# Opening and first batch: queries' exponentials head by head with row sums, and the key fold placed later

## The chip, the cores and the metric

The kernel runs on one core of one Trainium2 chip. The metric is the time of one execution on the device in microseconds (us), the median over runs.

## The reference

One launch computes three layers for a batch of 8, with 8 heads, 576 positions and 64 elements per head (512 channels): a linear attention, a gated feed-forward layer with a mixing over positions, and a second layer with a low-rank mixing over positions and a wide feed-forward part.

```
q_s = exp(q - max(q, axis=-1));  q_s = q_s / (sum(q_s, axis=-1) + 1e-9)     # per row and head
k_s = exp(k - max(k, axis=2));   k_s = k_s / (sum(k_s, axis=2) + 1e-9)      # over positions
x = q_s @ (k_s.T @ v)                                                       # per head
h = gelu_tanh(x @ w_in);  u, v = halves of h                                # 512 -> 2 x 512
v_n = (v - mean) / sqrt(var + 1e-6) * g_ln                                  # per row
x = x + (u * (w_sg @ v_n + b_sg)) @ w_out
y = x + (U @ V).T mixed over positions
out = y + relu(y @ w_ch1) @ w_ch2                                           # 512 -> 2048 -> 512
```

The change touches only how `q_s` is made for the first two batches, and when the maximum over positions is taken for the keys of the second.

## The kernel before, in words

A batch is worked on in tiles of 128 positions (four of 128 and one of 64, `t` = 0 to 4). Matrix products are done in split precision: each operand is a high part (`h`, written by ScalarE as a copy) and a low part (`l`, the rest, written by VectorE or GpSimd), and a product is three matmuls.

Names: `qt` and `kt` are the query and key tiles of a batch; `qm` and `qs` the row maxima and row sums of the queries per head; `km` the maximum of the keys over the tiles (`k_fold`), which four TensorE transposes (`pm`) and a reduction turn into `mx` (`k_max`), and four more (`pb`, `k_spread`) spread over all partitions. `k_sub` subtracts it, `k_exp` takes the exponential. `pk` is the product of keys and values (`emit_kv`), `pt` the transposed queries (`emit_qT`, which gives `qh`, `ql`), `px` the attention's output (`emit_xT`: `xh`, `xl`). `pv` is the gated layer's second half (`emit_Vh`, gelu into `ge`, of which there are three buffers; then the row statistics and the normalization, `vh`, `vl`), `pu` its first half in four blocks `f` (`emit_Uh`, gelu into `ut`), `pS` the mixing over positions in four blocks (`emit_S`, into `gt`, split into `gh` and `gl`), `py` the output product (`emit_y`). `pt`, `px`, `pv`, `pu`, `pS` and `py` share three PSUM buffers in turn.

The weights come as float64 words, are loaded in pieces into `stg`, clamped (L171), scaled by ScalarE (L177), merged by VectorE (L183, L184) and split into high and low parts (`wih`/`wil`, `wo_h`/`wo_l`). Some pieces are put between the steps of every batch.

The orders: in the opening (first batch up to `px`) VectorE, ScalarE, GpSimd and SyncE work in the order of the code. In the loop over the batches TensorE and VectorE do; ScalarE and GpSimd get theirs from a scheduler at build time. In the pass of the loop for batch `b`, the queries and keys of batch `b` + 1 (`nxt`) are prepared: maxima behind the `pv` products (`Q_MAX`, `FOLDS`), subtractions behind the `pu` products (`Q_SUB`, `K_SUB`), exponentials after the fourth gelu of `pu`, sums and the division (`q_total`, `q_norm`: two tiles on VectorE and three on GpSimd for the second batch) before the first `pS`; then `pk`, two `pt` and the first `py` follow `pS` on TensorE.

Of the kernel before, what the change touches and what calls it, by code (L numbers as in the profile page):

```python
# [22 lines left out]
def fused_kernel(tc, q, k, v, w_in, g_ln, w_sgT, b_sg, w_out, U, V, w_ch1, w_ch2, outT):  # L23
# [30 lines left out]
    def tt(eng, out, a, b, op):  # L54
        return eng.tensor_tensor(out=out, in0=a, in1=b, op=op)  # L55
# [347 lines left out]
    def k_fold(b):  # L403

        kt = k_t[b]
        m = km_t[b] = att.tile([P, C], F32, tag="kh", name="km")
        tt(dve, m, kt[:, 0], kt[:, 1], ALU.max)
        yield
        for t in range(2, NT):
            yield tt(dve, m, m, kt[:, t], ALU.max)  # L410
        tt(dve, m, m, kt[:, NT], ALU.max)
        yield

    def k_max(b):
# [23 lines left out]
        for t in tiles:  # L438
            act.activation(kt[:, t], kt[:, t], AF.Exp)

    q_s = {}

    def q3(t):
        return qt[0 : TR[t], t].rearrange("p (h d) -> p h d", d=D)

    def q_max(b, t):
        if t == 0:
            q_s[b] = tmpp.tile([P, NT + 1, H], F32, tag="qm", name="qm")
        dve.tensor_reduce(
            out=q_s[b][0 : TR[t], t], in_=q3(t), op=ALU.max, axis=mybir.AxisListType.X  # L450
        )

    def q_sub(b, t, eng=dve):
        n = TR[t]
        tt(eng, q3(t), q3(t), q_s[b][0:n, t].unsqueeze(2).to_broadcast([n, H, D]), ALU.subtract)

    def q_exp(b, t):
        act.activation(qt[0 : TR[t], t], qt[0 : TR[t], t], AF.Exp)

    def q_sum(b, t):  # L460
        if t == 0:
            q_s[b] = tmpp.tile([P, NT + 1, H], F32, tag="qs", name="qs")
        s = q_s[b]
        dve.tensor_reduce(out=s[0 : TR[t], t], in_=q3(t), op=ALU.add, axis=mybir.AxisListType.X)

    def q_total(b):

        s = q_s[b]
        for part in (s[:, 0:NT], s[0:R, NT]):
# [29 lines left out]

    def norm_kv(b):  # L500
        pk = kv_t[b]
        rs = tmpp.tile([P, 16], F32, tag="rs", name="rs")[:, 0:NC]
        for rows, _, _, total, _ in PAIR:
            dve.tensor_scalar(
                out=rs[rows].unsqueeze(2), in0=pk[rows, :, total], scalar1=1e-9, scalar2=None, op0=ALU.add
            )
        dve.reciprocal(out=rs, in_=rs)
        for rows, keys, _, _, rest in PAIR:
            tt(dve, kv[rows, :, keys], pk[rows, :, rest], rs[rows].unsqueeze(2).to_broadcast([E, NC, E]), ALU.mult)
        kh = att.tile([P, NC, P], F32R, tag="kh", name="kh")  # L510
# [682 lines left out]
    K_SUB = (((), (), (0, 1, 2), (3, 4)), ((), (), (0,), (1, 2, 3, 4)))  # L1193
    Q_NORM_DVE = (2, 5)

    def borrowed(tag):
# [3 lines left out]
    with in_order(dve, act, pool, sp):  # L1200
        load_k(0)
        load_q(0)
        ahead = list(pieces)
        for piece in ahead[0:1]:
            piece.load()
        load_v(0)
        for piece in ahead[1:5]:
            piece.load()
        for piece, tag in zip(ahead[5:14], ("vh0", "vl0", "vh1", "vl1", "vh2", "vl2", "vh3", "vl3", "vh4")):
            piece.load(borrowed(tag))  # L1210
        sp.dma_start(gl, g_ln)
# [42 lines left out]
    for b in range(B):  # L1254
# [53 lines left out]
        for f in range(NF):  # L1308
            if nxt and f == spread_at:
                k_spread(nxt)  # L1310
            if b == 0:
                slot(TURNS[b][1][f])
            if not nxt:
                for _ in range((0, 2, 2, 2)[f]):
                    next(prep, None)
            emit_Uh(b, f)
            if f == 0:
                emit_ln(b, NT)
# [17 lines left out]
        if nxt:  # L1336
            with contextlib.nullcontext() if b else tc.issue_after(last['g', 3].ins):
                for t in range(NT + 1):
                    q_exp(nxt, t)
            with contextlib.nullcontext() if b else tc.issue_after(last['g', 3].ins):  # L1340
                k_exp(nxt)
            for t in range(NT + 1):
                q_sum(nxt, t)
            q_total(nxt)
            for t in range(NT + 1):
                q_norm(nxt, t, dve if t < Q_NORM_DVE[b > 0] else pool)
# [170 lines left out]
```

## Time and profile before

| | |
|---|---|
| median of 3 runs | 1309.66 us (1308.72 to 1312.9) |
| the profiled execution | 1311.05 us, of it 1309.2 us span from the first to the last instruction |
| TensorE busy | 1260.0 us, 96% of the span; granted clock 0.991 of full speed on average |
| VectorE, ScalarE, GpSimd busy | 969.0, 636.9 and 330.4 us |
| opening, up to the last `px` | 0 to 36.4 us |
| first pass of the loop: `pv`, `pu`, `pS`, `pk`/`pt`, `py` | from 36.4, 58.8, 74.9, 89.9 and 95.7 us |

Times of instructions are counted from the start of the span. A row of the timeline gives start and duration of one instruction, or of several alike that follow one another (x2), and in brackets the idle time of the engine before it and whose end it waited for. The durations come from the profiled execution, whose time is 1.4 us above the median.

### The profile page before, as it was taken

The page shows a single profiled execution, that of the slowest core. Times are in us where ns is not written, and L with a number is a line of the kernel's source. Part 1 is how long each engine was busy: PE and PEld are TensorE (multiplying, and loading weights), DVE is VectorE, ACT ScalarE, POOL GpSimd, SP SyncE. Part 2 cuts the span into 40 slices and gives each one's busy share as a digit, 9 for nine tenths or more (in the row PEclk, how much of TensorE's full clock was granted, in tenths as well). Part 3 has the DMA queues.
Part 4 walks back from the last instruction along what each step waited for, and adds up shares of the span by engine and source line. Part 5 has one row for each costly group of instructions (what it writes and reads, how often), then busy time and mean ns, then how long its engine had stood idle before and what let it go on. Part 6 is the DMA issues. An engine that isn't in the chain of part 4 may idle for free.

```text
span 1309.2 us, 20581 instructions
## 1 busy us (share of the span) xinstructions
PE 1260.0 (96%) x7592; PEld 1139.1 (87%) x7592; DVE 969.0 (74%) x1406; ACT 636.9 (49%) x979; POOL 330.4 (25%) x426
## 2 busy tenths in 40 slices
PE   4799999999999999898999999999999999999998
PEld 3598999999898989798888888888888889999998
DVE  7888879787988888788668953598337963694485
ACT  4756656575757466654454512444134422451342
POOL 4634152624243333665340202000010002000000
PEclk9899999999999999998999999999999999999999
DMA  8515171725343352468998667678756788899896
GB/s 268 164 47 171 37 218 37 225 70 167 96 151 120 111 168 73 162 208 299 312 344 315 227 231 257 209 242 290 257 193 226 243 285 297 269 304 315 260 290 215
DMA packets 135907, 274.14 MB, mean 209 GB/s; under 512 B 15232, under 2 KB 56704, under 8 KB 135808
## 3 DMA queue, kind: packets, MB, share of 16 engines
q1 hardware_dynamic: 135808, 272.84, 63.2%
q8 instruction: 60, 0.98, 0.3%
q14 instruction: 39, 0.32, 0.1%
HBM read 224.56 MB, written 48.23 MB: 208 GB/s over the span
## 4 chain that ended last, share of the span: by engine, by line
PE 79%; DVE 7%; DMA 4%; ACT 2%; issue 1%; POOL 1%; SPq 0%; DVEq 0%; ACTq 0%; POOLq 0%
PE mm L52 50%; PE pS L52 6%; PE pu L52 6%; PE pv L52 5%; PE py L52 5%; DMA stg<-in_w_ch_dram 1%; PE pm L52 1%; PE pp L52 1%; PE px L52 1%; PE pt L698 1%; DVE yt L55 1%; DVE f L183 1%; PE pk L52 1%; PE pt L527 1%; DMA wu<-wd 1%
## 5 line engine op out<-in xcount | busy, mean ns | idle before, releaser
L52 PE MATMUL mm<-oh,wu 128*128 128x512 f32 (+1 forms) x1120 | 320.7, 367 | 0.0
L52 PE MATMUL mm<-uh,wu 128*128 128x512 f32 (+1 forms) x1064 | 303.7, 366 | 1.9 <-DMA wu<-wd 1.1
L52 PEld LDWEIGHTS mm<-oh,wu 128*128 128x128 f32 x1120 | 207.0, 188 | 26.1
L52 PEld LDWEIGHTS mm<-uh,wu 128*128 128x128 f32 x1064 | 196.3, 188 | 26.4 <-issue 1.4
L52 PE MATMUL mm<-ol,wu 128*128 128x512 f32 (+1 forms) x560 | 205.7, 367 | 0.0
L61 ACT ACTIVATE oh<-h 128x1024 fp32r<-128x1024 f32 (+1 forms) x140 | 135.2, 973 | 124.8 <-PE mm L52 102.4
L52 PE MATMUL mm<-ul,wu 128*128 128x512 f32 (+1 forms) x532 | 194.9, 366 | 0.0
L55 DVE TENSOR_TENSOR ol<-h,oh 128x1024 fp32r<-128x1024 f32 (+1 forms) x140 | 155.4, 1113 | 40.9 <-ACT oh L61 40.1
L55 POOL TENSOR_TENSOR ust<-ust 128x1024 f32<-128x1024 f32 (+1 forms) x16 | 36.4, 2282 | 389.4 <-DMA ust<-u2d 348.8
L55 DVE TENSOR_TENSOR h<-mm,u 128x1024 f32<-128x1024 f32 (+1 forms) x57 | 63.3, 1111 | 87.8 <-PE mm L52 87.7
L52 PEld LDWEIGHTS mm<-ol,wu 128*128 128x128 f32 x560 | 105.2, 188 | 13.1
L55 DVE TENSOR_TENSOR u<-mm,u 128x1024 f32<-128x1024 f32 (+1 forms) x53 | 58.9, 1111 | 76.7 <-PE mm L52 71.3
L52 PEld LDWEIGHTS mm<-ul,wu 128*128 128x128 f32 x532 | 99.9, 188 | 12.1
L55 POOL TENSOR_TENSOR chw<-f,chw 128x256 fp32r<-128x256 f32 x98 | 78.9, 820 | 95.4 <-ACT chw L61 95.3
L55 DVE TENSOR_TENSOR h<-h,h 128x1024 f32<-128x1024 f32 (+1 forms) x80 | 88.9, 1112 | 0.0
L1041 ACT ACTIVATE h<-mm 128x1024 f32<-128x1024 f32 (+1 forms) x19 | 17.8, 938 | 130.8 <-PE mm L52 130.8
L1032 ACT ACTIVATE h<-h 128x1024 f32<-128x1024 f32 (+1 forms) x60 | 58.1, 969 | 33.9 <-DVE h L55 33.9
L61 ACT ACTIVATE chw<-f 128x256 fp32r<-128x256 f32 x112 | 42.6, 412 | 62.7 <-DVE f L184 23.1
L61 ACT ACTIVATE u<-mm 128x1024 f32<-128x1024 f32 (+1 forms) x24 | 22.5, 939 | 103.1 <-PE mm L52 86.9
L171 POOL TENSOR_SCALAR stg<-stg 128x256 f32<-128x256 f32 (+1 forms) x83 | 41.0, 496 | 99.7 <-DMA stg<-in_w_ch_dram 39.0
L52 PE MATMUL py<-gh,wo_h 128*128 128x288 f32 x256 | 57.6, 307 | 3.0 <-DVE gt L665 2.1
L52 PE MATMUL py<-gl,wo_h 128*128 128x288 f32 x256 | 56.0, 301 | 3.4 <-DVE gl L55 3.4
(165 smaller groups left out, 2650.2 us busy)
## 6 DMA issues: line engine op xcount, KB each, us to landing
wu<-wd SPq DMA_DIRECT2D x280, 512.0 KB, 4.4
wd<-chw SPq DMA_DIRECT2D x112, 256.0 KB, 3.6
stg<-in_w_ch_dram SPq DMA_DIRECT2D x64, 256.0 KB, 3.7
u2d<-yt SPq DMA_DIRECT2D x32, 288.0 KB, 2.4
vt<-in_v_dram SPq DMA_DIRECT2D x32, 256.0 KB, 6.7
qt<-in_q_dram SPq DMA_DIRECT2D x7, 1024.0 KB, 8.1
kt<-in_k_dram SPq DMA_DIRECT2D x7, 1024.0 KB, 6.1
res<-u2d SPq DMA_DIRECT2D x12, 512.0 KB, 5.3
```

Source lines behind the costliest of these rows:

```text
L52: pe.matmul(out, lhsT, rhs, start=first, stop=last, skip_group_check=onto)
L55: return eng.tensor_tensor(out=out, in0=a, in1=b, op=op)
L61: return act.activation(out, src, AF.Copy)
L171: eng.tensor_scalar(out=hi, in0=hi, scalar1=F64_MOST, scalar2=-F64_MOST, op0=ALU.min, op1=ALU.max)
L183: dve.tensor_scalar(out=b, in0=b, scalar1=3, scalar2=None, op0=ALU.logical_shift_left)
L527: pe.transpose(pt[:, t * P : (t + 1) * P], qt[:, t, c * P : (c + 1) * P], ident)
L698: pe.transpose(pt[0:n, c * P : (c + 1) * P], y_t[b][:, c, t * P : t * P + n], ident)
L1032: act.activation(h, h, AF.Relu)
L1041: act.activation(h_out(j, 11, n), bank, AF.Relu)
```

## The change

**In the opening**, the queries of tiles 2, 3 and 4 no longer go through a subtraction of the maximum, one exponential of 512 columns and a sum of VectorE: the maximum is taken with a negative sign, and ScalarE takes eight exponentials of 64 columns per tile, one for each head, with the negative maximum as bias and the row sum as accumulator output. Tiles 0 and 1 stay as they were. The divisions are done in two parts, the exponentials of tiles 3 and 4 stand behind those of the keys, the first `pt` is taken up between `kv` and its split, and the table of the exponential is loaded at the start.

**In the first pass of the loop**, all five tiles of the second batch's queries are done in this way (40 exponentials). The fold of the keys stands behind the first `pu` block, its transposes `pm` behind the third, `pb` behind the fourth, and the keys' subtractions behind that; the row sums' reciprocals and the division of the queries (`divide`) stand behind the third `pS` block on VectorE's list; and the last tile's normalization is taken up behind the second `pu` block. From the second pass on nothing is changed.

```diff
+    BY_HEAD = {0: (2, 3, 4), 1: (0, 1, 2, 3, 4)}
...
+        if by_head(b, t):
+            dve.tensor_reduce(out=o, in_=q3(t), op=ALU.max, axis=mybir.AxisListType.X, negate=True)
+        else:
+            dve.tensor_reduce(out=o, in_=q3(t), op=ALU.max, axis=mybir.AxisListType.X)
...
     def q_exp(b, t):
-        act.activation(qt[0 : TR[t], t], qt[0 : TR[t], t], AF.Exp)
+        if not by_head(b, t):
+            act.activation(qt[0 : TR[t], t], qt[0 : TR[t], t], AF.Exp)
+            return
+        n = TR[t]
+        for h in range(H):
+            x = q3(t)[:, h]
+            act.activation(
+                x, x, AF.Exp, bias=q_m[b][0:n, t, h : h + 1], accum_out=sums(b)[0:n, t, h : h + 1]
+            )
...
+        act.preload_act_table(AF.Exp)
         run(k_fold(0))
         for t in (0, 1):
             q_max(0, t)
-            q_sub(0, t, dve if t in (3,) else pool)
+            q_sub(0, t, pool)
             q_exp(0, t)
         k_max(0)
         for t in range(2, NT + 1):
             q_max(0, t)
-            q_sub(0, t, dve if t in (3,) else pool)
+        q_exp(0, 2)
         k_spread(0)
         for t in range(NT + 1):
             k_sub(0, t)
             k_exp(0, (t,))
-            if 0 < t < NT:
-                q_exp(0, t + 1)
         more(OP[0])
+        for t in range(3, NT + 1):
+            q_exp(0, t)
         emit_kv(0)
-        for t in range(NT + 1):
+        for t in range(2):
             q_sum(0, t)
-            if t == 2:
-                more(OP[1])
-        q_total(0)
-        for t in range(NT + 1):
+        q_total(0, 0, 2)
+        for t in range(2):
             q_norm(0, t, dve)
-            if t == 1:
-                more(OP[2])
-        norm_kv(0)
-        emit_qT(0, 0)
+        more(OP[1])
+        q_total(0, 2)
+        for t in range(2, NT + 1):
+            q_norm(0, t, dve)
+        def first_block():
+            more(OP[2])
+            emit_qT(0, 0)
+        norm_kv(0, first_block)
...
-    FOLDS = ((0, 1, 2, 1, 0), (0, 0, 2, 2, 0))
+    FOLDS = ((0, 0, 0, 0, 0), (0, 0, 2, 2, 0))
...
             emit_Uh(b, f)
+            if b == 0 and f == 0:
+                run(fold)
+            if f == (0 if b else 1):
+                emit_ln(b, NT)
...
+            if b == 0 and f == 2:
+                k_max(nxt)
...
         if nxt:
+            if b == 0:
+                k_spread(nxt)
+                for t in range(NT + 1):
+                    k_sub(nxt, t)
+                with tc.issue_after(last['g', 3].ins):
+                    k_exp(nxt)
             with contextlib.nullcontext() if b else tc.issue_after(last['g', 3].ins):
                 for t in range(NT + 1):
                     q_exp(nxt, t)
...
         for f in range(NF):
             emit_S(b, f)
+            if b == 0 and f == 2:
+                divide(nxt)
```

The built programs show how the lists of the engines move. First ScalarE's list at its beginning, the opening; `wih1` are high parts of the weights of `pv`. Before:

```order
L458 ACT_TABLE_LOAD
L458 ACTIVATE qt_160<-qt_160 128x512 x2
L439 ACTIVATE kt_180<-kt_180 128x512 x2
L458 ACTIVATE qt_160<-qt_160 128x512
L439 ACTIVATE kt_180<-kt_180 128x512
L458 ACTIVATE qt_160<-qt_160 128x512
L439 ACTIVATE kt_180<-kt_180 128x512
L458 ACTIVATE qt_160<-qt_160 64x512
L439 ACTIVATE kt_180<-kt_180 128x512
L177 ACTIVATE f32_277<-stg_191 128x256
L177 ACTIVATE f32_325<-stg_204 128x256
```

and ScalarE's list at the same place in the changed program:

```order
L1235 ACT_TABLE_LOAD
L470 ACTIVATE qt_160<-qt_160 128x512 x2
L475 ACTIVATE qt_160,qs_255<-qt_160,qm_238 128x64 x8
L439 ACTIVATE kt_180<-kt_180 128x512 x5
L177 ACTIVATE f32_281<-stg_191 128x256
L475 ACTIVATE qt_160,qs_255<-qt_160,qm_238 128x64 x8
L475 ACTIVATE qt_160,qs_255<-qt_160,qm_238 64x64 x8
L177 ACTIVATE f32_347<-stg_204 128x256
L177 ACTIVATE f32_365<-stg_206 128x256
```

Three exponentials of 512 columns have become 24 of 64 columns; 16 of them stand behind the keys' five and ahead of the scaling of the second and third weight pieces.

Second, ScalarE's list behind the fourth gelu of `pu` in the first pass (`ut`). Before:

```order
L645 ACTIVATE ut_713<-pu_842 128x576
L458 ACT_TABLE_LOAD
L458 ACTIVATE qt_160<-qt_160 128x512 x4
L458 ACTIVATE qt_160<-qt_160 64x512
L61 ACTIVATE wo_h_168<-f32_796 128x256
L439 ACTIVATE kt_498<-kt_498 128x512 x2
L177 ACTIVATE f32_944<-stg_793 128x256
L439 ACTIVATE kt_498<-kt_498 128x512 x3
L61 ACTIVATE gh_898<-gt_929 128x576
```

and now:

```order
L667 ACTIVATE ut_719<-pu_850 128x576
L475 ACT_TABLE_LOAD
L475 ACTIVATE qt_160,qs_891<-qt_160,qm_534 128x64 x13
...
L439 ACTIVATE kt_516<-kt_516 128x512
L475 ACTIVATE qt_160,qs_891<-qt_160,qm_534 128x64 x14
L475 ACTIVATE qt_160,qs_891<-qt_160,qm_534 64x64 x8
L61 ACTIVATE wo_h_168<-f32_802 128x256
L177 ACTIVATE f32_978<-stg_799 128x256
L61 ACTIVATE wo_h_168<-f32_842 128x256
L61 ACTIVATE gh_932<-gt_963 128x576
```

The five exponentials of the queries are 40, and the first split of the mixing's result (`gh`) stands behind all of them and three weight steps.

Third, VectorE's list in the `pS` blocks of the first pass. Before, from the keys' subtraction on:

```order
L55 TENSOR_TENSOR kt_498<-kt_498,pb_826 128x512 x5
L464 TENSOR_REDUCE qs_883<-qt_160 128x8 x4
L464 TENSOR_REDUCE qs_883<-qt_160 64x8
L470 TENSOR_SCALAR qs_883<-qs_883 128x32
L471 RECIPROCAL qs_883<-qs_883 128x32
L470 TENSOR_SCALAR qs_883<-qs_883 64x8
L471 RECIPROCAL qs_883<-qs_883 64x8
L55 TENSOR_TENSOR qt_160<-qt_160,qs_883 128x512 x2
L665 SCALAR_TENSOR_TENSOR gt_929<-pS_900,gl_162,bb_163 128x576
```

and now, from the second block's result on:

```order
L55 TENSOR_TENSOR gt_1013<-gt_1013,ut_719 128x576
L55 TENSOR_TENSOR gl2_933<-gt_963,gh_932 128x576
L183 TENSOR_SCALAR f32_978<-f32_978 128x256
L184 SCALAR_TENSOR_TENSOR f32_978<-stg_799,f32_978 128x256
L55 TENSOR_TENSOR wo_l_169<-f32_969,wo_h_168 128x256
L687 SCALAR_TENSOR_TENSOR gt_1056<-pS_1027,gl_162,bb_163 128x576
L55 TENSOR_TENSOR gt_1056<-gt_1056,ut_719 128x576
L491 TENSOR_SCALAR qs_891<-qs_891 128x32
L492 RECIPROCAL qs_891<-qs_891 128x32
L491 TENSOR_SCALAR qs_891<-qs_891 64x8
L492 RECIPROCAL qs_891<-qs_891 64x8
L55 TENSOR_TENSOR qt_160<-qt_160,qs_891 128x512 x2
```

The sums are gone from VectorE's list, and reciprocals and division stand behind the third `gt` and behind the low part of the first one (`gl2_933`), which needs `gh`.

## Rows read from the trace of the kernel before

**Rows 1.** The page's first part: busy time, share of the span, instructions

```profile
PE 1260.0 (96%) x7592; PEld 1139.1 (87%) x7592; DVE 969.0 (74%) x1406; ACT 636.9 (49%) x979; POOL 330.4 (25%) x426
```

**Rows 2.** Windows by stage: start:end, length, busy by engine, PEclk, DMA share, GB/s

```profile
51.70:58.80 7.10, 0.01 (x1) 0.01 (x1) 6.86 (x15) 5.43 (x12) 4.69 (x5) 0.65 0.00 0
58.80:64.00 5.20, 5.20 (x22) 5.20 (x23) 4.71 (x12) 3.80 (x9) 2.36 (x3) 0.50 0.17 54
74.90:89.90 15.00, 15.00 (x115) 14.83 (x114) 14.75 (x29) 9.96 (x19) 7.30 (x7) 1.00 0.22 68
95.70:110.90 15.20, 14.25 (x105) 13.82 (x106) 14.38 (x34) 7.88 (x21) 5.49 (x8) 1.00 0.40 104
110.90:115.50 4.60, 4.44 (x36) 4.20 (x34) 2.16 (x4) 3.48 (x8) 2.66 (x3) 1.00 1.01 328
```

**Rows 3.** Timeline of TensorE, first pass: `pv`'s end to `py`

```profile
58.79 1.11 PE L419 MATMUL pm<-ident,km 128*128 128x128 f32 x4 [7.09 <-DVE km L55]
...
74.87 0.43 PE L52 MATMUL pS<-sg_h,vh 128*128 128x288 f32 x2
...
89.87 2.55 PE L52 MATMUL pk<-vt,kt 128*64 128x65 f32 x80
...
95.72 0.50 PE L52 MATMUL py<-gh,wo_h 128*128 128x288 f32 x2 [2.05 <-DVE gt L665]
```

**Rows 4.** ScalarE's groups by shape, whole span: busy us, mean ns

```profile
L623 ACT ACTIVATE ge<-ge,sh,mv 128x512 f32<-128x512 f32 x32 | 26.0, 814 | 17.2 <-DVE sh L620 17.2
L439 ACT ACTIVATE kt<-kt 128x512 f32<-128x512 f32 x40 | 22.3, 619 | 2.2 <-DVE kt L55 2.1
L61 ACT ACTIVATE wo_h<-f 128x256 fp32r<-128x256 f32 x8 | 3.3, 410 | 3.5 <-DVE f L184 3.5
```

**Rows 5.** Timeline of ScalarE, opening

```profile
7.62 1.28 ACT L458 ACT_TABLE_LOAD   x1 [7.62 <-DMA qt<-in_q_dram]
9.50 0.63 ACT L458 ACTIVATE qt<-qt 128x512 f32<-128x512 f32 x1 [0.59 <-POOL qt L55]
...
17.48 1.07 ACT L177 ACTIVATE f<-stg 128x256 f32<-128x256 f32 x3
...
25.75 0.63 ACT L61 ACTIVATE kh<-kv 128x512 fp32r<-128x512 f32 x1 [6.61 <-DVE kv L55]
```

**Rows 6.** Timeline of VectorE, opening and first pass

```profile
22.42 1.88 DVE L55 TENSOR_TENSOR qt<-qt,qs 128x512 f32<-128x512 f32 x3
...
52.34 1.82 DVE L55 TENSOR_TENSOR km<-km,kt 128x512 f32<-128x512 f32 x2
...
71.88 2.49 DVE L55 TENSOR_TENSOR qt<-qt,qm 128x512 f32<-128x512 f32 x4
...
79.27 3.04 DVE L464 TENSOR_REDUCE qs<-qt 128x8 f32<-128x512 f32 x5
...
94.76 0.82 DVE L665 SCALAR_TENSOR_TENSOR gt<-pS,gl,bb 128x576 f32<-128x576 f32 x1
```

**Rows 7.** Timeline of ScalarE, first pass: gelu of `pv`, fourth gelu of `pu`, exponentials

```profile
58.53 0.58 ACT L600 ACTIVATE ge<-pv 128x512 f32<-128x512 f32 x1
...
75.07 0.65 ACT L645 ACTIVATE ut<-pu 128x576 f32<-128x576 f32 x1 [2.97 <-PE pu L52]
75.74 1.28 ACT L458 ACT_TABLE_LOAD   x1
77.03 2.72 ACT L458 ACTIVATE qt<-qt 128x512 f32<-128x512 f32 x5
...
81.32 1.66 ACT L439 ACTIVATE kt<-kt 128x512 f32<-128x512 f32 x3
```

**Rows 8.** Timeline of GpSimd, first pass

```profile
55.24 1.29 POOL L55 TENSOR_TENSOR vl<-ge,vh 128x512 fp32r<-128x512 f32 x1 [0.80 <-ACT vh L61]
...
66.01 0.74 POOL L55 TENSOR_TENSOR wil<-f,wih 128x256 fp32r<-128x256 f32 x1
...
82.86 4.80 POOL L55 TENSOR_TENSOR qt<-qt,qs 128x512 f32<-128x512 f32 x3 [1.75 <-DVE qs L470]
```

More of the change, by code (lines that the diff above doesn't have):

```diff
@@ L439, in k_exp, with by_head @@
             act.activation(kt[:, t], kt[:, t], AF.Exp)
-    q_s = {}
+    q_m, q_s = {}, {}
+    BY_HEAD = {0: (2, 3, 4), 1: (0, 1, 2, 3, 4)}
+    def by_head(b, t):
+        return t in BY_HEAD.get(b, ())
     def q3(t):
@@ L447, in q_max, with sums, q_total @@
         if t == 0:
[L448 to L451, printed above, removed]
+            q_m[b] = tmpp.tile([P, NT + 1, H], F32, tag="qm", name="qm")
+        o = q_m[b][0 : TR[t], t]
+        if by_head(b, t):
+            dve.tensor_reduce(out=o, in_=q3(t), op=ALU.max, axis=mybir.AxisListType.X, negate=True)
+        else:
+            dve.tensor_reduce(out=o, in_=q3(t), op=ALU.max, axis=mybir.AxisListType.X)
     def q_sub(b, t, eng=dve):
         n = TR[t]
-        tt(eng, q3(t), q3(t), q_s[b][0:n, t].unsqueeze(2).to_broadcast([n, H, D]), ALU.subtract)
-    def q_exp(b, t):
-        act.activation(qt[0 : TR[t], t], qt[0 : TR[t], t], AF.Exp)
+        tt(eng, q3(t), q3(t), q_m[b][0:n, t].unsqueeze(2).to_broadcast([n, H, D]), ALU.subtract)
+    def sums(b):
+        if b not in q_s:
+            q_s[b] = tmpp.tile([P, NT + 1, H], F32, tag="qs", name="qs")
+        return q_s[b]
+    def q_exp(b, t):
+        if not by_head(b, t):
[7 more added lines that the diff above has]
+            )
     def q_sum(b, t):
-        if t == 0:
-            q_s[b] = tmpp.tile([P, NT + 1, H], F32, tag="qs", name="qs")
+        s = sums(b)
+        if not by_head(b, t):
+            dve.tensor_reduce(out=s[0 : TR[t], t], in_=q3(t), op=ALU.add, axis=mybir.AxisListType.X)
+    def q_total(b, first=0, end=NT + 1):
         s = q_s[b]
[L464 to L469, printed above, removed]
+        parts = [s[:, first : min(end, NT)]] if first < NT else []
+        if end > NT:
+            parts.append(s[0:R, NT])
+        for part in parts:
             dve.tensor_scalar(out=part, in0=part, scalar1=1e-9, scalar2=None, op0=ALU.add)
@@ L498, in emit_kv, with norm_kv @@
         kv_t[b] = pk
-    def norm_kv(b):
+    def norm_kv(b, between=lambda: None):
         pk = kv_t[b]
@@ L509, in norm_kv @@
             tt(dve, kv[rows, :, keys], pk[rows, :, rest], rs[rows].unsqueeze(2).to_broadcast([E, NC, E]), ALU.mult)
+        between()
         kh = att.tile([P, NC, P], F32R, tag="kh", name="kh")
@@ L1189, in fused_kernel @@
     Q_MAX = (((0, 1), (2, 3), (), (4,), ()), ((0, 1, 2), (3,), (4,), (), ()))
-    FOLDS = ((0, 1, 2, 1, 0), (0, 0, 2, 2, 0))
+    FOLDS = ((0, 0, 0, 0, 0), (0, 0, 2, 2, 0))
     Q_SUB = (((0, 1), (2, 3, 4), (), ()),) * 2
     Q_SUB_POOL = ((3,), ())
-    K_SUB = (((), (), (0, 1, 2), (3, 4)), ((), (), (0,), (1, 2, 3, 4)))
+    K_SUB = ((), (), (0,), (1, 2, 3, 4))
     Q_NORM_DVE = (2, 5)
@@ L1248, in fused_kernel, with divide @@
             more(OP[5 + c])
+    def divide(b):
+        for t in range(NT + 1):
+            q_sum(b, t)
+        q_total(b)
+        for t in range(NT + 1):
+            q_norm(b, t, dve if t < Q_NORM_DVE[b > 1] else pool)
     gate.append(nc.cur_bb.bb.instructions[-1])
@@ L1291, in fused_kernel @@
                     emit_PV(b - 1, c)
-        spread_at = 2 if b else 3
+        spread_at = 2 if b else NF
         if nxt:
-            k_max(nxt)
+            if b:
+                k_max(nxt)
         else:
@@ L1322, in fused_kernel @@
                     next(prep, None)
-            if nxt:
+            if b == 0 and f == 2:
+                k_max(nxt)
+            if nxt and b > 0:
                 for t in Q_SUB[b > 0][f]:
                     q_sub(nxt, t, pool if t in Q_SUB_POOL[b > 0] else dve)
-                for t in K_SUB[b > 0][f]:
+                for t in K_SUB[f]:
                     if f >= spread_at:
@@ L1336, in fused_kernel @@
         if nxt:
+            if b == 0:
+                k_spread(nxt)
+                for t in range(NT + 1):
+                    k_sub(nxt, t)
+                with tc.issue_after(last['g', 3].ins):
+                    k_exp(nxt)
             with contextlib.nullcontext() if b else tc.issue_after(last['g', 3].ins):
@@ L1339, in fused_kernel @@
                     q_exp(nxt, t)
-            with contextlib.nullcontext() if b else tc.issue_after(last['g', 3].ins):
+            if b > 0:
                 k_exp(nxt)
[L1342 to L1346, printed above, removed]
+            if b > 0:
+                divide(nxt)
         if not nxt:
@@ L1354, in fused_kernel @@
             emit_S(b, f)
+            if b == 0 and f == 2:
+                divide(nxt)
             if not nxt:
```

1 line of the change is left out of this document (removed).

## The prediction

> **What bounds the kernel now.** I read the page's busy times first, then the windows by stage, then the timelines of the engines around each gap of TensorE. TensorE is busy for 1260.0 of 1309.2 us [rows 1], so a change that adds no matmul can give back at most its 49 us of gaps, and it can open new ones. The change moves instructions in the first 115 us alone; behind that the lists of the engines are the same but for a few neighbours on ScalarE. So the question is what happens to the gaps up to 115 us, and whether the rest only shifts.
>
> The largest gap of the first pass lies between `pv` and `pu`: 7.10 us without a matmul, and then 5.2 us at a granted clock of 0.50, that is 1.2 GHz, before the clock is back at 2.4 GHz [rows 2]. What ends last there is the keys' fold: `pm` waits 7.09 us for `km` [rows 3], and two of the fold's steps alone hold VectorE from 52.34 for 1.82 us [rows 6]. `pS` begins at 74.87 and runs its 15.0 us without a gap [rows 2, 3]. Then `pk`, two `pt`, a wait of 2.05 us, and `py` at 95.72 [rows 3]. That wait is for VectorE, which is busy for 14.75 of the 15.0 us of `pS` [rows 2]; there it holds the subtractions (2.49 us) and the sums (3.04 us) of the queries [rows 6]. From 95.7 to 115.5 TensorE is busy for 14.25 + 4.44 = 18.7 of 19.8 us [rows 2], so a delay of `py` comes through but for about 1.1 us. In the opening ScalarE has a hole of 6.61 us before `kh` [rows 5].
>
> **The price of a head.** An exponential of 64 columns with bias and row sum does not occur before. From the groups by shape: 512 columns take 619 ns and 256 take 410, so 0.82 ns a column; 64 columns would take 253. Two operands from memory make 814 out of 619, so 97 ns each [rows 4]: 350 ns with the bias. Five exponentials in a row take 2.72 us [rows 7], so 525 ns from one start to the next, 94 less than the duration: 256 ns a head. What the sum adds is unknown. Lower bound: nothing, 0.256 us. Upper bound: an empty instruction more (410 - 209 = 201 ns) with no overlap at all, 0.55 us. I take 0.35 us: writing a sum is nearest to one more operand in memory, 97 ns. The 24 heads of the opening then take 8.4 us in place of 1.6, the 40 of the first pass 14.0 in place of 2.7 [rows 7].
>
> **Opening.** ScalarE's two exponentials of tiles 0 and 1 stay bound by GpSimd [rows 5]; the heads of tile 2 start at about 11.0 and end at 13.8, the keys' five at 16.5, one scaling, and the 16 heads of tiles 3 and 4 end at 22.4. On VectorE one subtraction and three sums go (2.7 us), and the reciprocals of tiles 2 to 4 wait for 22.4. From there the row of before gives 0.7 us of reciprocals and 1.88 us of three divisions [rows 6], so 25.0 against 24.3. Behind it, on VectorE's list, stands one weight merge (0.7 us) more than before, since the scaling of its piece [rows 5] now follows the heads. Of these 1.4 us the small waits for `qh` take some 0.4: `pv` ends 1.0 us later. With 0.256 us a head it ends 1.0 us earlier, with 0.55 us 5.9 us later. Loading the table first I cost at nothing: the load ends at 8.90, and the exponential behind it starts at 9.50 because GpSimd's subtraction was not done [rows 5]. The Trainium skill, in ScalarE: Activation LUTs, What ACT_TABLE_LOAD costs, puts a switch of tables at about 2.66 us with its drain; by that the load would have held the first exponential to 10.28, and loading early would be worth 0.8 us. The trace does not agree: the later load takes 1.28 us from 75.74, and the first exponential starts at 77.03 [rows 7].
>
> **From `pv` to `pS`.** The first `pu` block follows `pv` at once. The second does not: its PSUM buffer is that of the fourth `pv` tile, which is free when that tile's gelu is done, at 59.1 before [rows 7]. That gelu needs the `ge` buffer of tile 0, free with its `vl` at 56.5 [rows 8]. Without the folds (1.82 us) ahead of it on VectorE, and with `vh` of tile 1 (0.5 us) now ahead of it on ScalarE, it ends at about 57.8. TensorE waits from 54.9 to 57.8. The third block's last weight piece is GpSimd's `wil`, done at 66.75 before [rows 8]; the chain through the last tile's gelu moves up by some 2.6 us, so 64.2, and that block ends at 65.0. `pm` follows when the four folds behind the last statistics are done, at about 65.1. The fourth block ends at 68.9, and `pb` waits for `mx`, which stands on VectorE's list behind the last tile's split and a weight split: `pS` begins at 70.0, against 74.87. That is -4.9 us, and it holds both the shorter gap and the matmuls that no longer run at 1.2 GHz. Behind `pm` is queued the rest of `pu`, behind `pb` all of `pS`.
>
> **From `pS` to `py`.** Let S be its start. The fourth gelu ends 0.5 us before S; the table load adds 1.3, the keys' exponentials 5 x 0.525 = 2.6, the heads 14.0: ScalarE is through at S + 17.4. Before, this was done at 82.98, S + 8.1 [rows 3, 7]. Only then come three weight steps and the first `gh`, 1.7 us. VectorE, which keeps its order, waits for that `gh`, and behind it stand the low part, a merge, a weight split, the third `gt` and the reciprocals, 4.0 us: S + 23.1. GpSimd divides three tiles, 4.80 us before [rows 8]: S + 27.9. With the last transposes `py` starts at S + 28.4, where it was 95.72 - 74.87 = S + 20.85 [rows 3]: +7.5 us. The removed 5.5 us of VectorE buy nothing here, since it now waits for ScalarE. With 0.256 us a head this is +3.7, with 0.55 us +15.5.
>
> **Clock.** `pk` ends at S + 17.5, and TensorE has nothing until VectorE's two divisions at about S + 24.4. That is as long as the gap of 7.10 us, behind which the clock was at 0.50 for 5.2 us [rows 2], worth 2.6 us; part of it falls on transposes that wait anyway: +2.0. Bounds 0 and 2.6.
>
> **Sum.** +1.0 - 4.9 + 7.5 + 2.0 = +5.6, less 1.0 us that the gaps between 95.7 and 115.5 take up: +4.6 us. The profiled execution took 1311.05 us, 1.85 of it around the span, and would be 1315.7; that execution is 1.4 us above the median, so the prediction is 1309.66 + 4.6 = 1314.3 us, 0.35% slower.
>
> **Rivals.** (a) The row sum costs nothing, 0.256 us a head: -1.0 - 4.9 + 3.7 and a clock loss of 0 to 2.0, less 0.7 taken up: -2.9 to -0.9, 1306.8 to 1308.8 us, not slower. It speaks for this that the sum needs no pass over the data of its own, against it that every operand in memory costs here [rows 4]. A microsecond a head weighs about 56 us (40 and two thirds of 24), so it decides below 0.27 us a head. (b) The sum is written by a step that does not overlap, 0.55 us a head: +5.9 - 4.9 + 15.5 + 2.0 - 1.0 = +17.5, 1327 us; with half of that step, 0.45 us, 1320. For it: a running sum is complete only after the last column. (c) The division is hidden: the late `divide` works because the chain behind the heads is shorter than I make it. GpSimd's three divisions took 4.80 us while VectorE was busy, and VectorE's took 1.88 us for three [rows 6, 8]; if they take 3.1 us, and the `gh` waits little, `py` starts at S + 25 and the clock stays: 1.0 - 4.9 + 4.1 - 1.0 = -0.8, and with a `pu` stage that loses no wait at all (S at 66.2 instead of 71.0) -5.6: 1304 to 1309 us. Against it: VectorE's list has a wait at `gh` that nothing gets around. (d) The change does nothing: the gap moves from ahead of `pu` to ahead of `py` nearly one for one; this is my forecast with 0.32 us a head, +2.9 us, 1312.6.
>
> **How the numbers follow.** Some 3.9 us, 0.3%, is what a measurement of this kernel can tell from no change. The forecast's sum at 0.31 to 0.40 us a head has a chance of 0.43, its own range is 1311 to 1318 and it falls on both sides of 1313.6, the bound of slower (0.25 slower, 0.17 same, 0.01 faster), with (d) in it; (a) 0.16 (0.04 faster, 0.11 same, 0.01 slower); (b) 0.17, all slower; (c) 0.24 (0.22 faster, 0.02 same). Together 0.27 faster, 0.30 same, 0.43 slower. The range leaves out the upper half of (b) and the far end of (c): 1304.5 to 1322 us.
>
> **What would show it.** Right: heads about 0.35 us apart on ScalarE; `pS` beginning at 70 to 72; ScalarE busy without a gap from there for some 17 us; VectorE idle ahead of the first low part of `gt`; TensorE idle for over 6 us ahead of `pt`, and a granted clock near 0.5 behind it; `py` at 98 to 100. Wrong: heads at 0.27 us or less; a granted clock that stays at 1.0 behind `pk`; `pu` blocks that follow one another without a wait; or, the other way, a wait of `pb` for `mx` of more than 2 us, or the granted clock falling in the wait ahead of the second `pu` block, which would cost up to 2.6 us more.

## The result, and the profile after

The changed kernel takes 1317.53 us (median of 14 runs, 1316.03 to 1325.48), the kernel before, run beside it, 1309.66 us: a ratio of 1.0065, 95% interval 1.0051 to 1.0078, so 0.65% slower by the ratio and 7.9 us by the medians, 3.2 us above the forecast of 1314.3 and inside its range.

The page's first part, to be read beside [rows 1]:

```profile
PE 1263.7 (96%) x7592; PEld 1141.1 (87%) x7592; DVE 963.7 (73%) x1395; ACT 653.1 (50%) x1099; POOL 327.4 (25%) x423
```

VectorE has 5.3 us less to do and ScalarE 16.2 us more, in 120 more instructions. Where that lands is seen in windows of the changed kernel by stage, cut at TensorE's waits (columns as in [rows 2]):

```profile
52.43:58.39 5.96, 3.33 (x25) 3.10 (x23) 3.60 (x12) 5.91 (x13) 3.98 (x6) 0.96 0.02 4
58.39:61.42 3.03, 3.03 (x12) 3.03 (x13) 2.89 (x10) 2.34 (x5) 1.44 (x2) 0.51 0.09 8
61.42:73.66 12.24, 9.49 (x70) 8.79 (x69) 10.26 (x16) 6.13 (x12) 5.82 (x6) 1.00 0.12 42
73.66:88.75 15.09, 15.09 (x116) 14.92 (x113) 8.46 (x16) 15.06 (x73) 1.26 (x3) 1.00 0.28 89
88.75:97.59 8.84, 2.55 (x82) 2.44 (x81) 4.69 (x12) 6.60 (x26) 3.02 (x4) 0.88 0.08 19
97.59:103.37 5.78, 3.05 (x10) 1.89 (x11) 5.02 (x5) 0.68 (x2) 4.54 (x3) 0.50 0.01 3
```

In the 15.09 us of `pS` ScalarE is busy throughout and VectorE for 8.46 us; before it was VectorE that was full there, with 14.75 [rows 2]. The 5.96, 12.24, 8.84 and 5.78 us windows hold TensorE's new waits. Its timeline shows them one by one, against [rows 3]:

```profile
58.39 0.85 PE L52 MATMUL pu<-xh,wih 128*128 128x288 f32 x2 [2.63 <-ACT ge L622]
...
67.21 0.53 PE L52 MATMUL pu<-xh,wil 128*128 128x288 f32 x2 [1.10 <-POOL wil L55]
69.37 0.66 PE L419 MATMUL pm<-ident,km 128*128 128x128 f32 x4 [1.63 <-DVE km L55]
...
73.66 0.52 PE L52 MATMUL pS<-sg_h,vh 128*128 128x288 f32 x2
...
97.59 0.99 PE L549 MATMUL pt<-ident,qt 128*128 128x128 f32 x2 [6.29 <-DVE qt L55]
99.67 0.47 PE L549 MATMUL pt<-ident,qt 128*128 128x128 f32 x1 [1.10 <-POOL qt L55]
...
103.37 0.83 PE L52 MATMUL py<-gh,wo_h 128*128 128x288 f32 x2
```

The one wait of 7.09 us ahead of `pm` has become three, 2.63, 1.10 and 1.63 us, and `pS` starts 1.21 us earlier. Then `py` starts 29.71 us behind `pS` where it was 20.85: 7.65 us later in all, and the second batch's `pv` starts at 123.10 instead of 115.46, also 7.64 later. The profiled span is 6.3 us longer, so the rest of the program takes up little.

What holds `py` is read from the other engines' timelines of the changed kernel. ScalarE's, from the fourth gelu on and at the end of the heads:

```profile
73.27 0.65 ACT L667 ACTIVATE ut<-pu 128x576 f32<-128x576 f32 x1 [2.18 <-PE pu L52]
73.94 1.28 ACT L475 ACT_TABLE_LOAD   x1
75.23 0.35 ACT L475 ACTIVATE qt<-qt,qm 128x64 f32<-128x64 f32 x1
75.49 0.19 ACT L475 ACTIVATION_READ_ACCUMULATOR qt<-qt,qm 128x1 f32 x1
75.58 0.33 ACT L475 ACTIVATE qt<-qt,qm 128x64 f32<-128x64 f32 x1
...
91.03 0.19 ACT L475 ACTIVATION_READ_ACCUMULATOR qt<-qt,qm 64x1 f32 x1
91.12 0.40 ACT L61 ACTIVATE wo_h<-f 128x256 fp32r<-128x256 f32 x1
...
92.06 0.67 ACT L61 ACTIVATE gh<-gt 128x576 fp32r<-128x576 f32 x1
```

VectorE's, from the late fold to the reciprocals:

```profile
63.55 5.77 DVE L55 TENSOR_TENSOR km<-km,kt 128x512 f32<-128x512 f32 x3
...
78.51 0.76 DVE L55 TENSOR_TENSOR gt<-gt,ut 128x576 f32<-128x576 f32 x1
...
92.75 0.87 DVE L55 TENSOR_TENSOR gl<-gt,gh 128x576 fp32r<-128x576 f32 x1 [9.75 <-ACT gh L61]
...
96.08 0.17 DVE L491 TENSOR_SCALAR qs<-qs 128x32 f32<-128x32 f32 x1
```

and GpSimd's, the division of three tiles:

```profile
96.71 5.42 POOL L55 TENSOR_TENSOR qt<-qt,qs 128x512 f32<-128x512 f32 x3 [1.17 <-DVE qs L491]
```

Read in order: the heads end 17.5 us behind the start of `pS`; the first `gt` was there at 79.3 us, but its `gh` is done only at 92.7; VectorE has stood still for 9.75 us for it; its list then needs 3.3 us to the reciprocals, GpSimd 5.42 us for its tiles, and `py` follows.

### The profile page after: what moved, and what is told of

Read it like the earlier page. It is cut to its first block, busy times and chain, and to the rows that moved or that the text cites. A ratio compares the mean times of both kernels' runs of the same rounds, so it can differ in the third digit from the quotient of the medians.

```text
span 1315.5 us, 20692 instructions
## 1 busy us (share of the span) xinstructions
PE 1263.7 (96%) x7592; PEld 1141.1 (87%) x7592; DVE 963.7 (73%) x1395; ACT 653.1 (50%) x1099; POOL 327.4 (25%) x423
## 4 chain that ended last, share of the span: by engine, by line
PE 77%; DVE 9%; ACT 6%; DMA 3%; POOL 2%; issue 2%; SPq 0%; DVEq 0%; POOLq 0%; ACTq 0%
PE mm L52 50%; PE pS L52 6%; PE pv L52 6%; PE pu L52 5%; PE py L52 4%; ACT qt L475 2%; DMA stg<-in_w_ch_dram 1%; DVE yt L55 1%; PE pp L52 1%; PE pt L720 1%; DVE f L183 1%; PE px L52 1%; PE pm L52 1%; DVE ul L55 1%; PE pk L52 1%
## 5 line engine op out<-in xcount | busy, mean ns | idle before, releaser
L52 PE MATMUL pu<-xh,wih 128*128 128x288 f32 x256 | 57.5, 306 | 3.2 <-ACT ge L622 2.6
```

The source lines that it names most:

```text
L52: pe.matmul(out, lhsT, rhs, start=first, stop=last, skip_group_check=onto)
```

## The experiments

All ratios are to the kernel before, run on the same chip. Times are the starts of TensorE's first `pv`, `pS`, `py` and the second batch's `pv` in each profile's timeline. "Division" is where the queries' reciprocals and division stand on VectorE's list.

| kernel | ratio, 95% interval | `pv` | `pS` | `py` | `pS` to `py` | second `pv` |
|---|---|---|---|---|---|---|
| before | 1 | 36.42 | 74.87 | 95.72 | 20.85 | 115.46 |
| the change | 1.0065 (1.0051 to 1.0078) | 37.67 | 73.66 | 103.37 | 29.71 | 123.10 |
| open_only | 1.0005 (0.9991 to 1.0018) | 38.22 | 76.10 | 96.52 | 20.42 | 116.01 |
| no_open | 1.0070 (1.0050 to 1.0090) | 37.40 | 75.90 | 105.86 | 29.96 | 126.10 |
| no_heads | 1.0019 (1.0004 to 1.0033) | 36.96 | 76.13 | 96.45 | 20.32 | 116.16 |
| no_places | 1.0079 (1.0058 to 1.0099) | 37.52 | 75.50 | 105.32 | 29.82 | 126.57 |
| no_accum | 1.0028 (1.0016 to 1.0041) | 37.61 | 74.56 | 99.15 | 24.59 | 119.28 |
| two_tiles | 1.0040 (1.0026 to 1.0054) | 37.13 | 75.81 | 101.30 | 25.49 | 120.97 |
| gh_early | 1.0064 (1.0050 to 1.0078) | 38.09 | 76.61 | 106.27 | 29.66 | 126.18 |
| divide_first | 1.0045 (1.0031 to 1.0059) | 37.24 | 74.89 | 101.05 | 26.16 | 122.36 |
| one_tile | 0.9999 (0.9983 to 1.0015) | 37.10 | 74.21 | 96.37 | 22.16 | 116.94 |
| folds_early | 1.0121 (1.0107 to 1.0135) | 37.25 | 74.23 | 103.09 | 28.86 | 124.79 |
| pm_late_ge4 | 1.0012 (0.9999 to 1.0025) | 36.89 | 79.22 | 98.61 | 19.39 | 119.25 |
| after_ge4 | 1.0066 (1.0053 to 1.0080) | 37.22 | 75.00 | 104.97 | 29.97 | 125.33 |

**Which part of the change costs.** Four kernels take the change apart.

> The opening of the change alone; the loop over the batches is as before. Theory H (ScalarE's 40 exponentials by head in the first pass hold `gh` and the division): the opening moved the end of `pv` by 0.7 us, so 1309.5 to 1311.5 us, the same as before. Rival O (the opening, with the lower granted clock behind its first transposes, costs most of it): 1313.5 us or more. Rival P (the late fold, `pm` and `pb` cost it) agrees with H here.

```diff
-    BY_HEAD = {0: (2, 3, 4), 1: (0, 1, 2, 3, 4)}
+    BY_HEAD = {0: (2, 3, 4)}
...
```

> The change without its part in the opening. H: 1316 to 1317.5 us, at most 1.5 us less than the whole change. O: 1313.5 us or less. P: as H.

```diff
-    BY_HEAD = {0: (2, 3, 4), 1: (0, 1, 2, 3, 4)}
+    BY_HEAD = {1: (0, 1, 2, 3, 4)}
...
```

> The change without the exponentials by head in the first pass: the second batch's queries are subtracted, exponentiated in 512 columns, summed and divided where before did it; the late places of the keys' fold, `pm`, `pb` and the last tile's normalization stay, and so does the opening. H: ScalarE is through 8 us behind the start of `pS` again, `py` starts at 95.5 to 98 us, 1310 to 1312.5 us. P: the late places alone make it slower, 1315 us or more, with `pS` as early as 74 us and a `pb` or `pm` that waits.

```diff
-    BY_HEAD = {0: (2, 3, 4), 1: (0, 1, 2, 3, 4)}
+    BY_HEAD = {0: (2, 3, 4)}
...
-            if b > 0:
-                divide(nxt)
+            divide(nxt)
...
-            if b == 0 and f == 2:
-                divide(nxt)
```

> The change with the keys' fold, `pm`, `pb`, subtractions and the last tile's normalization where before had them; the exponentials by head, the late division and the opening stay. H: the gap of 7 us ahead of `pu` is back, `pS` starts at 72 to 75.5 us, `py` 29 to 30 us behind it, 1316 to 1320 us. P: 1312 us or less, since the folds lie beside `pv` again.

```diff
-    FOLDS = ((0, 0, 0, 0, 0), (0, 0, 2, 2, 0))
+    FOLDS = ((0, 1, 2, 1, 0), (0, 0, 2, 2, 0))
...
-        spread_at = 2 if b else NF
+        spread_at = 2 if b else 3
...
```

The opening alone is not told from before, and without it the loss is all there (1318.99 us, where I had expected 1317.5 at most): O falls. Without the heads of the first pass 0.46% of the 0.65 are gone and `pS` to `py` is 20.32 us; with them, and the fold where it was, it is 29.82 us. So H holds against O and P: the loss comes with the heads. no_heads also has the division back ahead of `pS`, so it does not tell the heads from the late division; the next kernels do. P is right in one thing: the late places bring nothing by themselves (1.0019). The gap ahead of `pu` is not closed by them but spread. Waits of TensorE in no_heads (what waited, for whom, us in total, how often, the longest):

```profile
PE pm L419 <- DVE km L55: 3.0, 1, 3.0
PE pu L52 <- ACT ut L667: 2.9, 1, 2.9
PE pu L52 <- POOL wil L55: 1.5, 1, 1.5
```

Together 7.4 us, against the one wait of 7.09 [rows 3].

**What a head costs, and which wait passes it on.** no_accum leaves the accumulator out, two_tiles has 16 heads instead of 40, gh_early and divide_first turn the order around.

> The whole change, but the 40 exponentials by head of the first pass have no accumulator output: the row sums of the second batch's queries are left out and the division uses 1. Theory H (ScalarE's heads set the end of the first pass): each head saves the 0.095 us step of its accumulator read, 40 x 0.095 = 3.8 us; `py` starts 25.5 to 26.5 us behind the start of `pS` where it was 29.7, TensorE's wait ahead of `pt` falls to about 2.5 us, and the time is 1311.5 to 1314 us. Rival D (the division behind the third `pS` block, on VectorE and GpSimd, sets the end whatever ScalarE does): `py` stays at 29 us or more and the time at 1316.5 us or more.

```diff
+            if b == 1:
+                pool.memset(sums(b), 1.0)
...
-            act.activation(
-                x, x, AF.Exp, bias=q_m[b][0:n, t, h : h + 1], accum_out=sums(b)[0:n, t, h : h + 1]
-            )
+            kw = {} if b else {"accum_out": sums(b)[0:n, t, h : h + 1]}
+            act.activation(x, x, AF.Exp, bias=q_m[b][0:n, t, h : h + 1], **kw)
```

> The whole change, but in the first pass only tiles 0 and 1 of the second batch's queries by head; tiles 2 to 4 with a subtraction (where before had it), one exponential of 512 columns and a sum, this one at the late division. H: 24 heads of 0.33 us fewer and three exponentials of 0.525 us more, 6.3 us off ScalarE's chain; `gh` some 12 us behind the start of `pS`, VectorE's wait for it falls from 9.75 to 3 or 4 us, `py` 23 to 25 us behind `pS`, 1310 to 1313 us. D: the three sums make the late division 1.8 us longer, 1317 us or more.

```diff
-    BY_HEAD = {0: (2, 3, 4), 1: (0, 1, 2, 3, 4)}
+    BY_HEAD = {0: (2, 3, 4), 1: (0, 1)}
...
```

> The whole change, but ScalarE's list has the first `gh` ahead of the last 24 heads. H with the wait at `gh`: VectorE's low part, merge, weight split and third `gt` (some 4 us) are done while ScalarE still works on the heads; the reciprocals start 18 us behind the start of `pS` instead of 22.4, `py` 24.5 to 26 us behind it, 1311.5 to 1314 us. Rival E (all that counts is the end of the heads and what follows on ScalarE): VectorE's wait moves from `gh` to the reciprocals, the later `gh` come late, `py` at 28.5 us or more, 1316 us or more.

```diff
...
-                for t in range(NT + 1):
+                for t in range(NT + 1) if b else range(2):
...
             if f > 0:
-                split_G(b, f - 1)
+                high = split_G(b, f - 1)
+                if b == 0 and f == 1:
+                    with tc.issue_after(high.ins):
+                        for t in range(2, NT + 1):
+                            q_exp(nxt, t)
```

> The whole change, but the reciprocals and the division of the queries stand on VectorE's list behind the second `pS` block instead of the third, so ahead of everything that waits for a `gh` or a `wo_h` on ScalarE's list behind the heads. Theory L (what is lost besides the heads is VectorE's list: some 5 us of low part, merge, weight split and third `gt` between the end of the heads and the reciprocals): the reciprocals start about 17.7 us behind the start of `pS` instead of 22.4, GpSimd's division ends near 24, and `py` starts at 24.5 to 26 us instead of 29.7; the third and fourth `gt` come later, so TensorE waits 1 to 3 us inside the first `py` block; 1312.5 to 1316 us. Rival E (whatever stands behind the heads takes as long in any order): `py` at 28.5 us or more, 1317 us or more.

```diff
-            if b == 0 and f == 2:
+            if b == 0 and f == 1:
                 divide(nxt)
```

Without the accumulator 21 heads in a row take 5.14 us on ScalarE:

```profile
74.65 5.14 ACT L478 ACTIVATE qt<-qt,qm 128x64 f32<-128x64 f32 x21
```

That is 0.24 us from one to the next, against 0.33 with it (75.23 to 91.12 above holds 40 heads and five exponentials of the keys); `py` comes 24.59 us behind `pS`, 5.1 us earlier than with accumulators and 0.9 earlier than I expected. That is more than the 3.7 us of the reads; the granted clock from `pS` to `py` is also higher, 0.94 against 0.87 in the change, but what that gives was not told apart. D falls, since the late division is still there. In two_tiles VectorE waits 3.31 us for `gh`, as expected, and `py` comes at 25.49 us, 4.2 us earlier than in the change; I expected 23 to 25, and the ratio of 1.0040 (some 1315 us) is above my 1313.

gh_early is a miss of the experiment. The first `gh` is early, but `wo_h` of a weight piece still stands behind the heads on ScalarE's list, and VectorE's list comes to the `wo_l` that needs it before it comes to the reciprocals:

```profile
96.57 0.43 DVE L55 TENSOR_TENSOR wo_l<-f,wo_h 128x256 fp32r<-128x256 f32 x1 [7.47 <-ACT wo_h L61]
```

So it does not speak against L; it shows that one early result on ScalarE does not help a list that needs a second. divide_first passes both. The reciprocals then wait for the heads alone (VectorE's timeline, first for the sums of tiles 0 to 3, then of tile 4):

```profile
90.06 0.18 DVE L491 TENSOR_SCALAR qs<-qs 128x32 f32<-128x32 f32 x1 [5.83 <-ACT qt L475]
...
92.72 0.16 DVE L491 TENSOR_SCALAR qs<-qs 64x8 f32<-64x8 f32 x1 [2.09 <-ACT qt L475]
```

`py` comes 26.16 us behind `pS`, 3.5 us earlier. The later `gt` come late, as expected, and make the last two waits ahead of `py` (TensorE's timeline):

```profile
98.51 1.33 PE L549 MATMUL pt<-ident,qt 128*128 128x128 f32 x5 [1.60 <-DVE gt L687]
...
101.05 0.82 PE L52 MATMUL py<-gh,wo_h 128*128 128x288 f32 x2 [1.21 <-DVE gt L687]
```

Another 1.6 us are given back between `py` and the second `pv` (21.31 us, 19.73 in the change). TensorE waits no longer there than in the change, 0.37 us in both, but it is busy for 20.94 us instead of 19.36, at a granted clock of 0.87 instead of 0.94: `py` runs at half clock until 106.5, for over 5 us, where the change is back at full clock 2.4 us behind the start of `py`. The kernel is 1.0045. L holds: some 3.5 of the 8.9 us are the place of the division. The rest stands with the heads, since the reciprocals now wait for them alone; a kernel with the late division and no heads was not run.

> The kernel before, with one tile (the fifth) of the second batch's queries by head and nothing else of the change. ScalarE is busy for 12.8 of the 20.85 us from `pS` to `py` in before, and the first `gh` comes 10 us behind the start of `pS`. Theory H (heads cost only once they hold `gh` and the division): 8 heads, 2.6 us, fit ahead of `gh`; a subtraction and a sum of 0.6 us each leave VectorE; `py` 19.8 to 20.9 us behind `pS`, 1307.5 to 1310.5 us. Rival K (every tile by head costs a fifth of the whole loss, 1.6 us): 1311 us or more.

```diff
...
+    BY_HEAD = {1: (4,)}
...
                 for t in Q_SUB[b > 0][f]:
+                    if by_head(nxt, t):
+                        continue
...
```

With one tile by head the time is that of before (0.9999, 0.9983 to 1.0015): K would give 1.0012, which the interval does not quite exclude; `pS` to `py` is 22.16 us, 1.3 more than before and above what I expected, and `pv` to `pS` is as much shorter (37.11 us, 38.45 before).

**From `pv` to `pS`.** The forecast had 4.9 us of gain here.

> The kernel before, with two edits: TensorE's list has `pm` behind the second `pu` block instead of ahead of the first, and the fourth tile's gelu output takes a free buffer of `gt` in the first pass, so it need not wait for a `ge` buffer. No exponentials by head, no late fold. If the 7.1 us ahead of `pu` and the 2.6 us at half clock were lost for the order of `pm` and for the `ge` buffer: `pu` follows `pv`, `pS` starts at 67 to 71 us instead of 74.87, 1304 to 1307 us. If the weights' last low part (`wil`, GpSimd, near 66.5 us) sets the third `pu` block anyway: a wait of 4 us or more stands ahead of that block, `pS` at 71 to 74 us, 1307 to 1310 us.

```diff
+        if b == 0 and t == 3:
+            ge = tmpp.tile([P, S], F32, tag="gt", name="ge")[:, 0:F]
+        else:
+            ge = tmpp.tile([P, F], F32, tag="ge", name="ge", bufs=3)
...
-            k_max(nxt)
+            if b:
+                k_max(nxt)
...
             emit_Uh(b, f)
+            if b == 0 and f == 1:
+                k_max(nxt)
```

> The whole change, but the keys' fold lies beside `pv` again, as in before; `pm` and `pb` stay late. Theory F (the late fold, which took 5.77 us for three steps while GpSimd worked beside it, made `pm` wait and `pS` late): no wait ahead of `pm`, from the end of `pv` to `pS` 18.5 to 20.5 us instead of 21.2 to 23.9, 1314 to 1316 us. Rival V (VectorE is busy for 17 of the 21 to 24 us from `pv` to `pS` and sets the end wherever its fold stands): the waits move ahead of the second `pu` block and of `pb`, 21 to 24 us again, 1316.5 us or more.

```diff
-    FOLDS = ((0, 0, 0, 0, 0), (0, 0, 2, 2, 0))
+    FOLDS = ((0, 1, 2, 1, 0), (0, 0, 2, 2, 0))
...
-            if b == 0 and f == 0:
-                run(fold)
```

> The whole change, but the fourth tile's gelu output takes a free `gt` buffer in the first pass, so that this gelu need not wait until GpSimd's `vl` of the first tile has freed a `ge` buffer. Theory B (the wait of 2.6 to 3.3 us ahead of the second `pu` block is for that buffer, and the part from `pv` to `pS` is late by it): the wait is below 0.5 us, the granted clock stays at 1.0 there, and `pS` starts 17.5 to 20 us behind the end of `pv` instead of 21.2 to 23.9; 1313 to 1315.5 us. Rival W (the weights' last low part, `wil`, near 67 us, sets the third `pu` block, and the late fold the transposes behind it): the wait is gone but stands ahead of the third block instead, 21 us or more from `pv` to `pS`, 1316 us or more.

```diff
+        if b == 0 and t == 3:
+            ge = tmpp.tile([P, S], F32, tag="gt", name="ge")[:, 0:F]
+        else:
+            ge = tmpp.tile([P, F], F32, tag="ge", name="ge", bufs=3)
```

Each takes one wait away and gets another. In pm_late_ge4 `pu` follows `pv` closely, but `pb` waits 4.91 us for `mx`, which stands late on VectorE's list (TensorE's timeline):

```profile
73.44 1.12 PE L429 MATMUL pb<-ident,mx 128*128 128x128 f32 x4 [4.91 <-DVE mx L421]
```

Five smaller waits ahead of it add up to 4.2 us, and `pS` starts at 79.22: both of my alternatives were wrong. In folds_early `pm` waits for nothing, but the second block waits 2.96 us, the third 2.05 and `pb` 0.91; `pS` starts 36.98 us behind the first `pv`, 35.99 in the change, as V had it. In after_ge4 the second block waits 0.48 us and the third not for `wil`, so B's buffer is what that wait was for; but then (TensorE's timeline)

```profile
68.31 1.12 PE L419 MATMUL pm<-ident,km 128*128 128x128 f32 x4 [4.57 <-DVE km L55]
```

the late fold is next, and the time is that of the change. F and B are each right on their wait and wrong on the time; W is right on the time and wrong on the place, which is `pm` and not the third block. The fold early and the fourth buffer in one kernel were not tried.

The 1326 us of folds_early have another source. It is 1.7 us behind the change at the second `pv`, but its span (1322.4 us) is 6.9 us longer: in the last batch ScalarE's list came out in another order, and TensorE has a wait there that the change does not have:

```profile
643.36 1.22 PE L52 MATMUL mm<-uh,wu 128*128 128x512 f32 x2 [3.72 <-DVE yt L55]
```

That the order is the cause was not tried. Among the other kernels the time from the second `pv` to the end differs by up to 4.6 us (1189.2 us in two_tiles, 1193.8 in open_only), so a few microseconds between two kernels are read from the first pass here and not from the whole time.

## Why the prediction was right, and what was mis-sized

The direction was right, and so was the mechanism that decides it: the heads hold the first `gh`, behind it VectorE's list holds the division, and the division holds `py`. 4.6 us were forecast and 7.9 measured. In the profile the second `pv` comes 7.64 us later, 3.0 more than forecast: 2.8 of them are gain that did not come between the end of `pv` and `pS` (2.1 us came, of 4.9), the rest is behind `pS`. Two signs named in advance were missed, `pS` at 70 to 72 us (73.66) and `py` at 98 to 100 (103.37), and two came, TensorE idle for 6.29 us ahead of `pt` and half clock behind it.

**Price of a head**: 0.35 us forecast, 0.33 measured, made of 0.24 for the exponential and 0.09 for a separate instruction that reads the accumulator. The estimate of one more operand, 97 ns, was close by luck: it is an instruction and not an operand. Rival (a), a free sum at 0.256 us a head, was no way to a faster kernel: no_accum has 0.24 and is still 0.28% slower. I had priced it with the 4.9 us that did not come. One slip in the working decides nothing: the opening's upper bound counts all its 24 heads, the 56 us for a microsecond a head only 16 of them, which is 1.6 us in (b).

**Opening**: +1.0 us forecast. The last `pv` ends 0.9 us later in the profile, of which 0.46 is already there in the first exponential (9.96 us against 9.50 [rows 5]); by the runs it costs nothing that can be told (open_only, 1.0005). The table loaded first ends at 2.00 us and the first exponential waits for GpSimd until 9.96, so it is worth nothing, as costed (ScalarE's timeline):

```profile
0.72 1.28 ACT L1235 ACT_TABLE_LOAD   x1 [0.72 <-PEq L1551]
9.96 0.63 ACT L470 ACTIVATE qt<-qt 128x512 f32<-128x512 f32 x1 [7.95 <-POOL qt L55]
```

The load of the first pass begins 0.02 us behind the gelu ahead of it and takes 1.28 us, and the first head starts 1.31 us behind the gelu's end. The Trainium skill (ScalarE: Activation LUTs, What ACT_TABLE_LOAD costs) gives about 2.66 us for a switch of tables with its drain; the trace again does not agree.

**From `pv` to `pS`**: this is the step that was mis-sized, -4.9 us forecast with `pS` at 71.0, and 73.66 in the profile. From the first `pv` to `pS` the change has 35.99 us, and no_open, gh_early, no_accum and divide_first, with the same steps up to there, have 38.50, 38.52, 36.95 and 37.65, against 38.45 before: 0.9 us of gain on average, and 2.5 in this profile alone. Three things were missed.

The first is the late folds. The four took 6.4 us (0.67 and 5.77), where the four of before took 3.2 (1.82 for two [rows 6], 0.71 and 0.67 for the others), so `pm`, forecast at 65.1, waits and starts at 69.37. GpSimd works beside them from 62.95 to 68.76 us:

```profile
63.77 1.75 POOL L55 TENSOR_TENSOR vl<-ge,vh 128x512 fp32r<-128x512 f32 x1
...
66.44 0.71 POOL L55 TENSOR_TENSOR wil<-f,wih 128x256 fp32r<-128x256 f32 x1
...
67.50 1.26 POOL L55 TENSOR_TENSOR vl<-ge,vh 128x512 fp32r<-128x512 f32 x1
```

The last three folds take 0.79, 1.68 and 3.22 us, and each ends 0.53 to 0.55 us behind the end of an instruction of GpSimd (63.81, 65.52 and 68.76). It is not always VectorE that loses: in before the last fold takes 0.67 us at 58.06, and GpSimd's `wil` beside it 1.66 us in place of some 0.74. The Trainium skill (SBUF — State Buffer, SBUF: two separate sides) has an operation of VectorE with two inputs in SBUF and one of GpSimd that reads SBUF exclude each other, and the one that starts first keeps the other out to its end. The trace agrees with the first half in the ends of the folds; the second it does not show, as the third fold's record begins at 66.09, ahead of that of `wil`, and ends behind it. No run here takes GpSimd's work away, so the cause is not shown by itself.

The second is `wil`, which ended at 67.15 us and not at 64.2. The third is TensorE's clock, which fell in the wait ahead of the second `pu` block, as the prediction had named among its signs of being wrong. It cost some 1.5 us: 12 matmuls took 3.03 us there, where no_open, at full clock, has 23 in 3.02 (last section).

**From `pS` to `py`**: +7.5 us and +2.0 for the clock, less 1.0 taken up, makes 8.5; 8.86 were measured to `py`, with the transposes ahead of it at 0.50 of the clock, and from `py` to the second `pv` the sum is unchanged (19.73 us, 19.74 before): `py` begins at half clock, and waits of 0.33 and 0.60 us that before had inside `py` are gone. ScalarE was through at S + 17.5 (17.4 forecast), the reciprocals were done at S + 23.2 (23.1 forecast), GpSimd's division, 5.42 us instead of 4.80, at S + 28.5 (27.9), and the last transposes, at half clock, put `py` at S + 29.7 (28.4, with the clock priced apart). These parts were right; the clock's 2.0 and the 1.0 taken up can only be checked in their sum. divide_first shows that the wait at `gh` is a part of it and no_accum that the heads are.

**Rivals**: (b) fell with the price of a head; (c) with 9.75 us of waiting at `gh`; (d), the gap moves, is nearest to what happened, but the gap ahead of `pu` did not go: its 7.09 us [rows 3] are still there as 5.36, and 6.29 us ahead of `pt` are new.

## What to carry to other kernels

Work taken off a full engine is worth only what the engine that gets it can do before its own next result is asked for: here one tile of 8 heads on ScalarE cost nothing that could be told, and it got five, in one block ahead of a split that VectorE's list needed. In a list that is kept in order, what counts is everything that it must pass: an early `gh` did nothing while a `wo_l` behind it still waited for the same engine. And before a gap is counted as gain, the next two waits behind it are to be priced, as here the waits that came in place of the 7.09 us added up to nearly as much or more: 5.36 us in the change, 7.4 in no_heads, 9.1 in pm_late_ge4.

## What the runs showed of the hardware

An activation with accumulator output is two records on ScalarE, the exponential (333 ns, next start 0.24 us later) and a read (187 ns, next start 0.09 us later).

TensorE's clock fell once between `pv` and `pS` in the change and in no_open, which wait the same there but for the third block (1.10 and 2.42 us), and in different places. In the change it was at 0.51 behind the wait of 2.63 us (the window from 58.39 above, 12 matmuls in 3.03 us) and at full speed behind that for `pm`:

```profile
69.37:73.00 3.63, 3.63 (x28) 3.62 (x28) 1.86 (x4) 1.67 (x3) 0.00 (x0) 1.00 0.00 0
```

In no_open it was the other way; windows behind the wait of 2.61 us and behind that for `pm`:

```profile
58.48:61.50 3.02, 3.02 (x23) 3.02 (x24) 2.88 (x10) 2.33 (x5) 1.45 (x2) 1.00 0.09 14
69.45:73.00 3.55, 3.55 (x15) 3.55 (x16) 1.79 (x4) 1.66 (x3) 0.00 (x0) 0.50 0.00 0
```

The same stretch of matmuls runs at 1.2 GHz in one and at 2.4 GHz in the other, behind waits of the same length, so the length of that wait alone does not tell whether the clock falls behind it.
